# Eleven block products in place of twelve for units one to four, with w1 paired with w2, scores masked on two other engines, and the later steps listed anew

## The chip, the cores and the metric

The kernel runs on one NeuronCore of one Trainium2 chip. The metric is the device time of one execution in microseconds (us); less is better. The engines are named as the profile names them: PE is TensorE's matmul, PEld its weight load, DVE is VectorE, ACT is ScalarE, POOL is GpSimd, SP is SyncE, whose queue issues nearly all DMAs.

## The reference

Two blocks in a row, all in fp32. First a delta rule attention over 4 batches, 8 heads, 768 tokens and head size 48. For each batch and head, with k normalised to k_n:

```python
for t in range(S):
    y[:, :, t] = einsum('bhd,bhde->bhe', q[:, :, t], state)
    v_old = einsum('bhde,bhd->bhe', state, k_n[:, :, t])
    state = state + beta * einsum('bhd,bhe->bhde', k_n[:, :, t], v - v_old)
```

Then, on x = y laid out as 3072 tokens by 384 features, a feed-forward block: `h = ((x @ w1) * (x @ w2)) @ w3`, `out = h @ w_out`, with w1 and w2 of 384 by 1024, w3 of 1024 by 1024 and w_out of 1024 by 384.

## The kernel before

The attention works in 12 chunks of 64 tokens. A chunk has steps with names: `k`, `v` and `p` load its inputs, `d` turns permuted tiles of k and q into features (four DVE transposes into `KQ`), `s` forms scores on PE and takes from them U (scaled) and PT (masked by `smask`), `e` forms the off-diagonal corner of the chunk's inverse, `c` is the chain through the state (R = v minus old, then X, then the state S), and `y` forms outputs and copies them with ACT into `xT`, from which six DMAs move the last sixteen features of each row group. Two chunks make a unit of 512 tokens, numbered 0 to 5. Once for each unit `g` and `N` form the norms of k, and `V` inverts the 32 by 32 diagonal blocks by 31 pairs of DVE operations (L439, L444) on `Vb`, `Ub` and `tb`.

The feed-forward block follows unit by unit. w3 @ w_out is folded into `w34` at the start (L758), so a unit needs x @ w1, x @ w2, their elementwise product `ab`, and `ab` @ `w34`. The `a` steps form the two products for one of eight blocks of 128 columns at a time: three matmuls of 128 by 512 for w1, an ACT copy from PSUM, three for w2, and a DVE multiply from PSUM (L778, L790, L794). Unit 0 does it by halves of the tokens (`a` and `b` steps). The `o` step multiplies `ab` by `w34` with Winograd's seven products for eight; `S` (capital) forms its sums of `ab` on POOL (L1004), `T` its sums of weights, and `x` adds the results up from PSUM and stores them (L1032, L1063).

Unit 5, the last, has no attention beside it. Its `E` step already forms x @ w1 and x @ w2 by eleven products in place of twelve (L897): tokens in two halves, K in three parts, and Winograd's scheme over the first two parts and two halves of the columns, separately for w1 and for w2. `G` forms its token sums on DVE (L880) and `W` its weight sums on POOL (L858).

The PSUM has four single banks in turn, tag `f` (`ps_f`, for the feed-forward block), and two double banks, tag `w` (`ps_w`, for the attention).

What sets the order of the work: every step is a generator, and `ORDER`, one long list of names written out by hand, says which generator goes one `yield` further. At the end `in_text_order` ties each engine's instructions to the order of this text. So all queues are fixed, an engine that waits holds up all that is listed behind it on that engine, and only semaphores between engines decide when things start.

Of the kernel before, what the change touches and what calls it, by code (L numbers as in the profile page):

```python
# [8 lines left out]
FP32 = mybir.dt.float32  # L9
# [31 lines left out]
beta P12 g0 P3 K0 g0 K0 g0 P13 K1 g0 P8 P12 g0 K1 K1 P11 P9 Q0 Q0 g0 Q0 P10 P12 g0 Q0 Q0 g0 k2  # L41
K1 s0 g0 P9 P10 P8 N0 K1 q1 P2 s0 N0 P3 Q1 s0 P12 p2 g1 Q1 P2 N0 s0 s0 Q1 P9 Q1 P8 Q1 g1 s0 P3
s0 t2 t2 t3 s1 P5 P8 P2 g1 s1 P2 P1 s1 s1 t3 P9 P5 s1 P4 s1 P5 u0 P5 s1 d2 P1 P4 t1 u1 t0 P6 t4
P7 t1 t10 P1 t0 t5 V0 t4 P14 g1 V0 P1 t10 P6 f1 t5 V0 d2 P4 P6 V0 V0 V0 P7 V0 P7 V0 P16 P14 V0
P4 V0 P19 P19 P19 P6 f0 P16 P17 P17 V0 V0 P16 V0 V0 P17 P7 f2 k3 P14 p2 V0 V0 v1 P19 P15 f1 f0
g1 f1 t11 V0 d2 t11 P15 f2 f5 V0 P14 P15 f0 P16 v0 P17 V0 V0 V0 V0 g1 P20 f5 V0 f2 f5 t6 t9 P15
t6 P20 t7 V0 n1 P22 P20 V0 t7 d2 s0 V0 V0 f3 P23 P20 P22 t8 P21 V0 n0 P24 n0 f3 V0 V0 n1 t8 V0
V0 t9 V0 V0 s2 p3 f4 f3 P23 P22 P26 g1 V0 g1 V0 f4 g1 P21 P22 P23 t14 d3 f4 P23 g1 t12 p3 V0 N1
P30 t12 t14 t15 e0 t15 d3 f7 d3 f6 e0 P30 P21 e0 e0 P24 f7 s2 s2 e1 e0 s2 P24 e0 e1 V1 p4 s2 e1
P26 s2 e1 P25 d3 c0 P21 P30 u2 s3 c0 s3 P26 N1 P31 P24 y0 s3 s3 y0 c0 s3 s3 P25 t13 N1 e1 u3 P31  # L50
c0 P26 P31 P32 c1 V1 c1 e1 P25 V1 P27 c1 V1 c1 V1 V1 t13 V1 V1 V1 V1 V1 V1 y0 V1 P25 f7 f6 f6
P30 P32 P32 v2 V1 P27 s1 P31 V1 V1 y1 b3 b1 V1 b0 P32 P28 y1 b1 V1 b1 b3 P29 P27 b2 b3 y1 V1 P27
b1 b0 P29 P29 c1 a01 b2 a03 P28 V1 a01 a00 b3 P28 P29 a02 a02 a03 P35 P28 V1 a05 b7 a00 V1 V1 V1
V1 a06 P33 V1 b5 a05 b7 b0 V1 P34 V1 b5 V1 a06 V1 V1 V1 P34 k4 V1 P35 V1 g2 a00 V1 k5 a00 b0 V1
V1 g2 a04 P34 n2 p4 n2 a07 c1 a04 b2 b4 P33 b6 b2 P35 V1 g2 g2 P34 g2 e2 a07 g2 P33 e2 P35 c2 c2
e3 d4 a03 d4 a03 a01 P33 g2 b4 d4 g2 e2 b6 e2 a07 e2 b4 d4 T a01 T b4 e2 a07 c2 s4 p5 g2 c2 T g2
N2 V2 b6 p5 b6 s4 b5 s4 c2 a06 c2 a06 a04 v3 y2 d5 b5 d5 k6 s4 e3 d5 s4 y2 a02 a05 d5 s4 b7 a04
n3 S0 a02 a05 S0 s5 S0 u4 e3 s5 n3 s5 e3 b7 T o0 c3 c3 s5 g3 s5 S0 N2 N2 x0 e3 g3 e3 o0 s5 c3 c3
u5 o0 x0 V2 S0 x0 y3 V2 y3 S0 V2 S0 V2 S0 S0 V2 V2 V2 S0 g3 o0 S0 o0 S0 x0 V2 c3 o0 v4 y3 V2 V2
V2 x0 p6 V2 x0 V2 S0 a10 a10 S0 g3 S0 x0 V2 x0 S0 o0 x0 x0 p6 a14 V2 k7 a17 a17 a14 V2 V2 V2 a15  # L60
a16 V2 a16 a15 V2 g3 V2 V2 V2 V2 V2 v5 V2 x0 a13 V2 V2 V2 a17 a12 V2 a13 g3 V2 V2 g3 a17 c3 a14
a13 d6 d6 a11 V2 e4 n4 a12 e4 e4 c4 d6 V3 e4 a14 a10 n4 g3 d6 c4 e5 a11 e4 s6 g3 a13 e4 a12 p7
a10 c4 g3 N3 s6 c4 s6 a11 y4 n5 y4 c4 e5 a12 c4 a11 a15 c5 n5 e5 p7 a16 d7 d7 d7 d7 o1 c5 v6 a16
k8 g4 g4 e5 g4 p8 a15 g4 s7 s7 S1 e5 s7 S1 e5 x1 s7 s7 S1 s7 c5 o1 s6 S1 u7 c5 o1 s6 s6 u6 S1 S1
V3 S1 y5 c5 c5 V3 V3 V3 V3 V3 o1 S1 x1 k9 S1 y5 S1 y5 o1 S1 S1 x1 x1 V3 S1 S1 V3 c6 V3 S1 S1 V3
d8 o1 x1 x1 v7 a20 n6 x1 V3 a20 o1 x1 a23 V3 V3 x1 V3 x1 n7 a27 a24 d8 a26 V3 V3 V3 V3 x1 g4 V3
a23 V3 a25 V3 a27 a27 V3 a24 V3 V3 a26 a20 V3 g4 V3 p8 V3 V3 V3 V3 p9 V3 V3 a25 d8 n6 d8 g4 a20
a22 a22 a24 V3 c6 a27 a25 a24 a21 a21 e6 e6 e6 g4 e7 N3 e6 a25 N3 g4 s8 g4 N4 s8 e6 a22 s8 a26
e6 c6 c6 N4 s8 a26 s8 y6 a22 V4 p9 N4 S2 d9 e7 s8 a21 e7 y6 u8 d9 a21 e7 c6 a23 d9 p10 e7 d9 S2
c6 S2 s9 n7 a23 s9 e7 o2 s9 c7 s9 S2 s9 k10 S2 c7 x2 o2 c7 S2 S2 o2 u9 s9 V4 c7 V4 S2 y7 V4 V4  # L70
x2 V4 g5 g5 V4 p10 d10 y7 S2 x2 S2 o2 y7 V4 o2 x2 c7 V4 V4 S2 S2 V4 o2 a35 x2 x2 k11 x2 S2 V4 x2
S2 a35 v8 V4 S2 V4 V4 S2 V4 x2 n8 o2 a37 x2 V4 v9 V4 V4 V4 x2 a34 n8 V4 V4 a36 a30 V4 V4 V4 V4
V4 a37 V4 a34 a33 V4 g5 a33 a30 a32 a36 V4 V4 V4 V4 a34 a33 V4 V5 a32 e8 n9 c7 e8 a30 c8 a33 e8
e9 e8 g5 a35 a34 c8 a30 e8 g5 d10 a32 e9 g5 a32 g5 a36 e8 e9 S3 c8 a36 a35 a31 d10 d10 e9 a31 n9
c8 g5 c8 c8 g5 g5 e9 a31 s10 N5 e9 p11 s10 s10 a31 c9 a37 a37 p11 c9 y8 N5 v11 d11 S3 d11 d11 o3
v10 d11 s10 y8 s10 S3 u10 S3 s11 N5 s11 o3 s10 c9 s11 c9 s11 S3 x3 S3 s11 o3 S3 S3 y9 o3 s11 x3
S3 o3 u11 V5 S3 S3 V5 y9 V5 x3 n11 S3 x3 V5 V5 V5 S3 y9 S3 S3 V5 c9 V5 o3 x3 V5 x3 x3 V5 V5 x3
S3 a47 o3 x3 V5 V5 a47 x3 V5 V5 a47 n10 V5 a46 a40 a40 V5 a47 V5 a43 V5 a46 x3 a42 a45 V5 a42 V5
a41 a45 a43 V5 V5 V5 V5 V5 V5 a44 V5 a44 V5 a45 a41 V5 V5 V5 V5 c9 W W W W W W W W a42 e10 a40
e10 n11 a42 e10 a44 e10 c10 a45 n10 e11 e10 e11 c10 a43 e10 c10 c10 a40 e11 a41 a46 e11 c10 a44  # L80
S4 a43 e11 a41 S4 c10 o4 e11 a46 c11 x4 S4 S4 y10 o4 c11 c11 S4 y10 S4 S4 S4 S4 S4 c11 o4 y11 o4
x4 S4 S4 S4 o4 y11 x4 x4 o4 S4 x4 x4 S4 y11 S4 x4 G5 x4 E5 x4 o4 x4 E5 x4 E5 E5 S5 E5 E5 S5 E5
E5 S5 o5 S5 S5 S5 o5 S5 S5 S5 x5 S5 S5 S5 o5 o5 x5 S5 S5 S5 o5 S5 o5 x5 x5 o5 x5 x5 x5 x5 x5 x5
x5 x5 x5 x5
# [4 lines left out]
def kernel(  # L89
# [54 lines left out]

    def two_banks():
        return in_turn(psW, [P, 2, 512], "w", 2, "ps_w")
# [44 lines left out]
    kperm, qperm = (padded(x, [P, B, NP, 2, BS], 1)[0] for x in ("kperm", "qperm"))  # L191
# [3 lines left out]

    def load_crossed(src, m, dma, tag, bufs):

        t = in_turn(work, [P, NR, H, D], tag, bufs, tag)
        for z in range(2):
            for e in range(2):  # L200
                dma(  # L201
                    out=t[half(z ^ e)].rearrange("t r (a e) d -> t e (r a) d", e=2)[:, e],
                    in_=src.rearrange("(z r) (a e) t d -> z e (r a) t d", z=2, e=2)[
                        z, e, :, C * m : C * m + C, :
                    ].rearrange("g t d -> t g d"),
                )
        return t
# [14 lines left out]
    def load_perm(m):  # L222
        for src, dst in ((k, kperm), (q, qperm)):
# [15 lines left out]

    beta_tok = const.tile([P, NCH, NR, H], FP32, name="beta_tok")  # L240
# [4 lines left out]
    def across(src, dst):  # L245

        n = src.shape[1]
        ps = bank([P, n, NR, NP])
# [3 lines left out]
        psv = ps[:].rearrange("p c r a -> p (c r) a")  # L252
# [10 lines left out]
    def squares(j):  # L263
# [9 lines left out]
        yield from across(ss[:, 1], ss[:, 0])  # L273

    def norms(j):
# [31 lines left out]
        yield from across(w[:, 0], w[:, 1])  # L307
# [10 lines left out]
    def by_vector(m):  # L318
        KQ = new_KQ(m)
        for i, src in enumerate((kperm, qperm)):  # L320
            for z in range(2):
                bs = slice(NR * z, NR * z + NR)
                dve.transpose(
                    out=KQ[:, bs, :, i, :].rearrange("p b a t -> p (b a) t"),
                    in_=src[:, bs].rearrange("p b a x d -> p (b a) (x d)"),
                )
                yield
# [28 lines left out]
    def scores(m):  # L356
        u = Us[m % 2][:, 0 : NR * H * C].rearrange("p (r h t) -> p r h t", r=NR, h=H)
        for r in range(NR):
# [30 lines left out]
            if m < 2:  # L389
# [66 lines left out]
    T22s = padded("T22", [P, NR, H, BS], 2)  # L456

    def from_blocks(m):
# [6 lines left out]
        T22 = T22s[m % 2]  # L465
# [9 lines left out]
    def corner(m):  # L475
        yield from from_blocks(m)
        TT, T22, U, T11 = TTs[m % 2], T22s[m % 2], Us[m % 2], T11s[0]
# [64 lines left out]
    def chain(c):  # L542
        TT, nv, KQ = TTs[c % 2], vtoks[c], KQs[c]
# [21 lines left out]
        def by_features(ps, r, h, z):  # L565
            g = NP * r + h // 2
            return ps[feat(h % 2), z, D * g : D * g + D]
# [5 lines left out]
        R = nv  # L573
        if c > 0:
# [4 lines left out]
            R = in_turn(work, [P, NR, H, D], "R", 1, "R")  # L579
            v3, r3 = (  # L580
                x[:].rearrange("p r (a e) d -> p (r a) e d", e=2) for x in (nv, R)
            )
            dve.tensor_tensor(
                out=r3, in0=v3, in1=ps.rearrange("p e g d -> p g e d"), op=ALU.subtract
# [7 lines left out]
        for e in range(2):  # L592
            dve.tensor_tensor(
                out=X[:].rearrange("p r (a e) d -> p e (r a) d", e=2)[:, e], in0=ps[:, e],
                in1=scale_of(ws, c, 1).rearrange("p r (a e) -> p e (r a)", e=2)[:, e]
                .unsqueeze(2).to_broadcast([P, H, D]),
                op=ALU.mult,
            )
        yield
        if c < NCH - 1:  # L600
            kt = ktoks[c]
            ps = products(
                by_features,
                lambda r, h, z: kt[half((z + h) % 2), r, h, :],
# [4 lines left out]
            for z in range(2):  # L609
                f = feat(z)  # L610
                if c == 0:
                    dve.tensor_copy(out=Sn[f], in_=ps[f])
                else:
                    dve.tensor_tensor(out=Sn[f], in0=St[f], in1=ps[f], op=ALU.add)
# [73 lines left out]

    CW = 512
# [119 lines left out]
    def weight_sums():  # L809
# [11 lines left out]
        U3 = room[4][:, 0:DM]  # L821
# [12 lines left out]
    w12_sums = {}  # L834

    def w12_weight_sums():
        for w, (s, res) in enumerate(
            (
                (w1s, [new_room(x, [P, BS, BS], 1) for x in ("Ub", "Vb")]),
                (w2s, [kperm, qperm]),  # L840
            )
        ):
            flat = [
# [361 lines left out]
```

## Time and profile before

| what | value |
|---|---|
| three plain runs | 590.34, 588.90, 587.33 us; median 588.9 |
| the profiled execution | span 592.1 us, mean granted PE clock 0.971 |
| PE busy | 540.8 us (91%) |
| PEld busy | 393.3 us (66%) |
| DVE busy | 378.9 us (64%) |
| ACT busy | 159.2 us (27%) |
| POOL busy | 192.8 us (33%) |
| DMA | 57.32 MB, mean 97 GB/s |

The span of the profiled execution is 3.2 us over the median of the plain runs; what lies around the span is not in the profile. A matmul of this kernel is two passes in the records (288 records of L778 for w2 are 144 matmuls), and the mean duration of one record is longer than the distance of two, since passes overlap; the chain of waits shows the distance. Busy shares are averages over a start in which weights come in and a long middle in which attention and feed-forward share PE, so stages are read apart.

### The profile page before, as it was taken

How to read it: one execution, taken by the hardware profiler on the slowest of the kernel's cores; microseconds unless marked ns; L12 is line 12 of the kernel's file. 1: busy time of each engine (PE TensorE's matmuls, PEld its weight loads, DVE VectorE, ACT ScalarE, POOL GpSimd, SP SyncE). 2: the span in 40 equal slices, each digit the busy share in tenths (PEclk: the TensorE clock that was granted, in tenths of full speed). 3: DMA queues.
4: the chain of work that ended last, by engine and by line, in shares of the span. 5: the costliest groups of instructions: out<-in, count | busy, mean ns of one | idle time of the engine just before them, and what ended most of it. 6: DMA issues, size and time to landing. Idle time of an engine off the chain costs nothing.

```text
span 592.1 us, 19305 instructions
## 1 busy us (share of the span) xinstructions
PE 540.8 (91%) x8268; PEld 393.3 (66%) x8268; DVE 378.9 (64%) x872; ACT 159.2 (27%) x337; POOL 192.8 (33%) x240
## 2 busy tenths in 40 slices
PE   2469889788989999999999989999999999999997
PEld 2456455667878874558854659644688445988897
DVE  3796897678986579674787544874855943325432
ACT  4666354453412202121210222011122112311100
POOL 7563543032453701207121025022051071501441
PEclk9879998779999999999999989999999999999999
DMA  9979997677857445563453344625332040010001
GB/s 245 198 163 268 196 182 140 127 162 154 133 78 101 99 83 107 83 98 56 113 99 75 56 64 86 125 60 78 58 64 79 27 89 4 3 41 27 1 1 53
DMA packets 219508, 57.32 MB, mean 97 GB/s; under 512 B 206656, under 2 KB 212800, under 8 KB 219424
## 3 DMA queue, kind: packets, MB, share of 16 engines
q1 hardware_dynamic: 215232, 55.31, 47.2%
q10 hardware_dynamic: 4192, 0.79, 1.0%
q8 instruction: 65, 1.06, 0.8%
q14 instruction: 19, 0.16, 0.1%
HBM read 43.88 MB, written 11.01 MB: 93 GB/s over the span
## 4 chain that ended last, share of the span: by engine, by line
PE 60%; SPq 15%; DMA 14%; DVE 6%; issue 3%; ACT 1%; POOL 0%; DVEq 0%; ACTq 0%
PE ps_f L778 29%; PE ps_f L1032 14%; SPq L229 6%; PE ps_w L550 4%; DMA raw<-in_moe_w_dram 4%; PE ps_f L897 3%; PE ps_w L651 3%; PE ps_w L897 3%; DMA Ub<-Ud 2%; DMA ktok<-in_k_dram 2%; PE ps_w L497 2%; SPq L201 2%; DMA Ud<-U 2%; DVE tb L439 1%; SPq L683 1%
## 5 line engine op out<-in xcount | busy, mean ns | idle before, releaser
L778 PE MATMUL ps_f<-xT,w2s 128*128 128x512 f32 (+1 forms) x288 | 112.2, 535 | 2.2 <-issue 2.2
L778 PE MATMUL ps_f<-xT,w1s 128*128 128x512 f32 (+1 forms) x288 | 107.0, 524 | 2.8 <-DMA xT<-xT 2.8
L1004 POOL TENSOR_TENSOR ab<-ab 128x256 f32<-128x256 f32 x96 | 67.0, 728 | 90.2 <-DVE ab L794 60.9
L778 PEld LDWEIGHTS ps_f<-xT,w1s 128*128 128x128 f32 x288 | 53.9, 190 | 48.7 <-issue 42.9
L778 PEld LDWEIGHTS ps_f<-xT,w2s 128*128 128x128 f32 x288 | 53.4, 191 | 44.6 <-issue 41.5
L1032 PE MATMUL ps_f<-w,ab 128*128 128x192 f32 x376 | 66.6, 330 | 0.2 <-issue 0.2
L1032 PEld LDWEIGHTS ps_f<-w,ab 128*128 128x128 f32 x376 | 61.1, 190 | 3.8 <-issue 2.9
L790 ACT COPY ab<-ps_f 128x512 f32<-128x512 f32 (+1 forms) x48 | 23.6, 517 | 130.9 <-PE ps_f L778 119.6
L439 DVE TENSOR_TENSOR tb<-Vb,Ub 128x31 f32<-128x31 f32 (+15 forms) x124 | 44.8, 361 | 19.6 <-DMA Ub<-Ud 16.3
L1032 PE MATMUL ps_f<-room,ab 128*128 128x192 f32 x272 | 48.0, 329 | 1.0 <-DVE room L1063 0.8
L444 DVE TENSOR_TENSOR Vb<-Vb,tb 128x31 f32<-128x31 f32 (+15 forms) x124 | 45.0, 363 | 4.3
L758 PE MATMUL ps_f<-w2s,w3T 128*128 128x384 f32 x128 | 45.8, 513 | 0.2 <-ACT w3T L752 0.2
L1032 PEld LDWEIGHTS ps_f<-room,ab 128*128 128x128 f32 x272 | 44.1, 190 | 1.8 <-issue 1.3
L672 ACT COPY xT<-ps_w 48x256 f32<-48x256 f32 x96 | 30.4, 365 | 55.0 <-PE ps_w L651 54.5
L269 POOL TENSOR_TENSOR sq<-ktok 128x384 f32<-128x384 f32 x24 | 20.7, 868 | 68.6 <-DMA ktok<-in_k_dram 62.3
L794 DVE TENSOR_TENSOR ab<-ab,ps_f 128x512 f32<-128x512 f32 (+1 forms) x48 | 27.7, 590 | 16.9 <-PE ps_f L778 16.7
L536 POOL TENSOR_TENSOR vtok<-vtok,n 128x384 f32<-128x384 f32 x24 | 20.3, 855 | 50.1 <-DMA vtok<-in_v_dram 50.1
L758 PEld LDWEIGHTS ps_f<-w2s,w3T 128*128 128x128 f32 x128 | 25.0, 201 | 16.9 <-issue 2.4
L366 PE MATMUL ps_w<-KQ 48*64 48x128 f32 x384 | 30.1, 293 | 1.7 <-DVE PT L396 1.7
L372 PE MATMUL ps_w<-KQ 48*64 48x64 f32 x768 | 30.5, 232 | 0.1
L714 POOL TENSOR_TENSOR w<-w,raw 128x512 uint32<-128x512 uint32 x16 | 20.8, 1305 | 27.7 <-ACT raw L707 9.0
L372 PEld LDWEIGHTS ps_w<-KQ 48*64 48x64 f32 x768 | 27.3, 145 | 0.3 <-ACT KQ L346 0.2
(155 smaller groups left out, 782.2 us busy)
## 6 DMA issues: line engine op xcount, KB each, us to landing
raw<-in_moe_w_dram SPq DMA_DIRECT2D x16, 512.0 KB, 6.5
vtok<-in_v_dram SPq DMA_DIRECT2D x24, 192.0 KB, 4.4
raw<-in_moe_w_dram SPq DMA_DIRECT2D x24, 192.0 KB, 4.6
out_dram<-osb SPq DMA_DIRECT2D x46, 96.0 KB, 2.3
ktok<-in_k_dram SPq DMA_DIRECT2D x44, 96.0 KB, 4.2
raw<-in_moe_w_out_dram SPq DMA_DIRECT2D x8, 384.0 KB, 4.4
Ud<-U SPq DMA_DIRECT2D x48, 64.0 KB, 3.2
Ub<-Ud SPq DMA_DIRECT2D x6, 512.0 KB, 3.9
```

Of the source, the lines that this page charges most:

```text
L229: sync.dma_start(out=dst[quarter(2 * e + j), :, :, tb, 0:nd].rearrange("t b a d -> t (b a) d"), in_=src.rearrange("b (a e) t d -> e (b a) ...
L366: pe.matmul(ps[half(z), 0, n : n + 128], lhsT=x[:, 0, :], rhs=x.rearrange("p j t -> p (j t)"), start=True, stop=True,)
L372: pe.matmul(ps[half(z ^ j), 1, n + C * j : n + C * j + C], lhsT=x[:, 0, :], rhs=x[:, j, :], start=True, stop=True,)
L439: dve.tensor_tensor(out=tv, in0=V[:, 0 : s + 1, s : s + 1].to_broadcast([P, s + 1, n]), in1=U[:, s, s + 1 : BS].unsqueeze(1).to_broadcast( ...
L444: dve.tensor_tensor(out=o, in0=o, in1=tv, op=ALU.subtract)
L672: act.copy(out=xT[f, p:NP:2, b : b + NR, cc, :].rearrange("p a r t -> p r a t"), in_=pyv[f, z, b : b + NR],)
L758: pe.matmul(ps[:, 0:DM], lhsT=w3Ts[jc, kc // 4][:, kc % 4 * P : kc % 4 * P + P], rhs=wo[:, kc], start=(kc == 0), stop=(kc == KF - 1),)
L778: pe.matmul(ps[:].rearrange("p b c t -> p b (c t)"), lhsT=w[:, m, js], rhs=x[:, m, :, c0:c1].rearrange("p b c t -> p b (c t)"), start=(m = ...
L794: dve.tensor_tensor(out=t, in0=t, in1=ps, op=ALU.mult)
L897: pe.matmul(acc[i, w, name], lhsT=w12_sums[w][b][:, P * i : P * i + P], rhs=x_sums[u][x], start=new, stop=True, skip_group_check=not new,)
L1004: pool.tensor_tensor(out=o_, in0=x_, in1=y_, op=op)
L1032: pe.matmul(ps[b][:, b, :], lhsT=abs_[u, HF * f + i][:, t0 : t0 + P], rhs=ws_[w][:, i], start=first and i == 0 and (b == 0 or n == "F"), s ...
```

## The change

Units 1 to 4 get the eleven products too, and unit 5 is done in the same way. The scheme's column halves are now w1 and w2 themselves: for each pair `p` of column blocks (256 columns), B11, B21 and L1 are taken from w1 and B12, B22 and L2 from w2. Each of the eleven products is two matmuls of 128 by 256, both into one full bank of 128 by 512 (A, B, C or D). A unit has four such pairs, and a pair has four generators: `a` (P1 into A, an ACT copy, P6 and P7 into B with a DVE add after each), `h` (two rounds into C, three DVE operations), `i` (D, a DVE add, a POOL multiply by `late`) and `j` (P2 and L1 into A). Token sums are formed by POOL and the weight sums, 16 operations of 128 by 256, too. `S` works on 512 columns, 8 operations for a unit in place of 16. `o` and `x` are split by bank.

Besides: PT of chunks 4 to 11 is no longer a DVE multiply from PSUM but an ACT copy and a POOL multiply by `smask` (as for chunks 0 and 1). The state update is one DVE operation of 128 by 768 in place of two of 48 by 768, X one in place of two, and R overwrites v. To find room, `kperm` and `qperm` become one `perm` from chunk 4 on, used for k and then for q, with `spare` and `x_room` beside it, and `T22` is one tile from chunk 4 on. `across` uses a double bank from unit 3 on. `ORDER` is unchanged up to the middle of `V1` and is listed anew from there.

```diff
+    def perms(m):
+        if m >= 4:
+            return perm, perm
+        return perm, spare[:].rearrange("p (b a x d) -> p b a x d", b=B, a=NP, x=2)
...
-            if m < 2:
+            if m < 2 or m > 3:
                 act.copy(out=by_parity(PT), in_=psv[:, :, :, 1, :])
                 yield
                 pool.tensor_tensor(
...
-            for z in range(2):
-                f = feat(z)
-                if c == 0:
-                    dve.tensor_copy(out=Sn[f], in_=ps[f])
-                else:
-                    dve.tensor_tensor(out=Sn[f], in0=St[f], in1=ps[f], op=ALU.add)
+            if c == 0:
+                dve.tensor_copy(out=Sn[:], in_=ps)
+            else:
+                dve.tensor_tensor(out=Sn[:], in0=St[:], in1=ps, op=ALU.add)
...
+    def w12_parts(p):
+        n = HB * P
+        c = slice(n * p, n * p + n)
+        B11, B21, L1 = (w1s[:, m, c] for m in range(KM))
+        B12, B22, L2 = (w2s[:, m, c] for m in range(KM))
...
+    def token_sums(u):
+        for o_, x, y, op in token_parts(u)[1]:
+            pool.tensor_tensor(out=o_, in0=x, in1=y, op=op)
+        yield
...
+            for k, (x, b) in enumerate(todo):
+                for i in range(2):
+                    pe.matmul(
+                        acc[name][:, n * i : n * i + n],
+                        lhsT=ws[b][:, P * i : P * i + P], rhs=xs[x],
...
+        def main():
+            skip("f")
+            products("A", ("P1", "P1"))
+            yield
+            for z in range(2):
+                halves[u, p, z] = slab("ab")[:]
+            act.copy(out=halves[u, p, 1], in_=acc["A"])
+            yield
+            products("B", ("P6", "P6"))
+            yield
+            plus(halves[u, p, 0], halves[u, p, 1], "B")
+            yield
+            products("B", ("P7", "P7"))
+            yield
+            plus(halves[u, p, 1], halves[u, p, 1], "B")
+            yield
+
+        def second():
+            products("C", ("P5", "P5"), ("A2", "L2"))
+            yield
+            plus(late[:], halves[u, p, 1], "C")
+            yield
+            products("C", ("P3", "P3"), ("S5", "L2"))
+            yield
+            Z0 = halves[u, p, 0]
+            plus(Z0, Z0, "C")
+            yield
+            dve.tensor_tensor(out=Z0, in0=Z0, in1=acc["A"], op=ALU.mult)
+            yield
+
+        def other():
+            products("D", ("P4", "P4"), ("A2", "L1"))
+            yield
+            Z1 = halves[u, p, 1]
+            plus(Z1, Z1, "D")
+            yield
+            eng = dve if (u, p) == (last, HF - 1) else pool
+            eng.tensor_tensor(out=Z1, in0=Z1, in1=late[:], op=ALU.mult)
+            yield
+
+        def first():
+            products("A", ("P2", "P2"), ("A1", "L1"))
+            yield
...
-            for i in range(HF):
+            for i in range(HF if u == 0 else HF // 2):
```

## The prediction

> **What bounds the kernel now.** I read the page first, then the windows, then the chain of waits, then the groups by form, and the timeline where a duration looked odd.
>
> ```profile
> PE 540.8 (91%) x8268; PEld 393.3 (66%) x8268; DVE 378.9 (64%) x872; ACT 159.2 (27%) x337; POOL 192.8 (33%) x240
> ```
>
> 91% for PE is a mean over two stages. The windows (window, its length, then busy us and instructions of PE, PEld, DVE, ACT and POOL, the granted PE clock, DMA share and GB/s) part the middle, from the fourth chunk's outputs to the twelfth's, from the last unit:
>
> ```profile
> 203.50:519.60 316.10, 310.86 (x5021) 204.52 (x5017) 198.92 (x464) 60.78 (x136) 79.62 (x105) 0.99 0.39 72
> 519.60:588.80 69.20, 67.34 (x356) 61.46 (x352) 27.18 (x64) 7.96 (x22) 17.55 (x25) 1.00 0.06 18
> ```
>
> In both PE is busy 97 to 98% of the time; DVE has 63% in the middle, POOL 25%. So from 203 us on the time is PE's work, and each us taken off PE is a us of the run, until another engine holds PE up. The chain of waits (start, us, what) gives the price of that work, in passes (two to a matmul):
>
> ```profile
> 249.66 2.77 PE ps_f L778 x6
> ...
> 292.75 2.57 PE ps_f L778 x6
> ...
> 343.38 2.25 issue
> 345.62 4.54 PE ps_f L778 x6
> ...
> 538.75 1.73 PE ps_w L897 x8
> ```
>
> A pass of 512 columns takes 2.57/6 = 428 ns in a row, one of 256 columns 1.73/8 = 216 ns. After a burst of the attention's small matmuls, six passes take 2.77: a restart costs 0.20 us. The third piece is a stop of PE for 2.25 us, and behind it six passes took 4.54 where they take 2.77. The groups by form give the other prices (line, engine, shapes and count, then busy us and mean ns):
>
> ```profile
> L778 PE MATMUL ps_f<-xT,w2s 128*128 128x512 f32 x192 | 89.2, 610 | 2.2 <-issue 2.2
> L778 PE MATMUL ps_f<-xT,w1s 128*128 128x512 f32 x192 | 84.8, 594 | 0.5 <-DMA xT<-xT 0.5
> L1004 POOL TENSOR_TENSOR ab<-ab 128x256 f32<-128x256 f32 x96 | 67.0, 728 | 90.2 <-DVE ab L794 60.9 <-PE ps_f L1032 22.3 <-DVE ab L917 7.0
> L794 DVE TENSOR_TENSOR ab<-ab,ps_f 128x512 f32<-128x512 f32 x32 | 21.5, 681 | 16.5 <-PE ps_f L778 16.3
> L614 DVE TENSOR_TENSOR S<-S,ps_w 48x768 f32<-48x768 f32 x20 | 18.9, 947 | 11.7 <-PE ps_w L550 9.8 <-PE ps_f L254 1.7
> L396 DVE TENSOR_TENSOR PT<-ps_w,smask 128x512 f32<-128x512 f32 x20 | 13.5, 678 | 1.9 <-PE ps_w L651 1.9
> L392 POOL TENSOR_TENSOR PT<-PT,smask 128x512 f32<-128x512 f32 x4 | 5.1, 1275 | 2.5 <-DMA kperm<-in_k_dram 2.4 <-ACT PT L390 0.2
> ```
>
> **The products: -12.3.** Units 1 to 4 lose 384 passes of 512 columns, 384 x 0.428 = 164.5 us, and get 4 units x 4 pairs x 11 products x 2 matmuls x 2 passes = 704 passes of 256 columns, 704 x 0.216 = 152.2 us. By the ratio of columns alone, 1/12 of 164.5, it is -13.7; I take the rows. Weight loads double, but at 190 ns each they fit under a pass of 216 in the last unit, where the passes are of this kind already. That the change does what it says is seen in the listing: 440 matmuls of 128 by 256 where there were 88.
>
> **Finer mixing: +3.8.** A block's products used to go in threes; now pieces of two or four matmuls of 128 by 256 lie between attention steps. Counted in the two kernels' PE order from the fourth chunk's outputs on, the feed-forward work restarts behind small matmuls 55 times, 36 before: 19 x 0.20 = 3.8. Bounds: 0, where the small matmuls' own tail hides it, and 3.8.
>
> **Waits for DVE inside a pair: +1.0.** New is that PE waits for DVE in the middle of a sum: P7 goes into B only when the add has read P6 (and that add needs the ACT copy of A), the second round into C only when `late` is formed. Behind the waiting matmul stands all of PE's queue, attention included. The nearest row is the last unit, which did this already with eight sets of sums (waited for, us in total, times, longest us):
>
> ```profile
> PE ps_f L897 <- DVE ktok L908: 0.3, 1, 0.3
> ```
>
> Walking a pair in unit 5's new listing: P7 goes 1.7 us behind P6 (the first round of C between them, 8 passes), and the add takes 0.68; C's second round goes behind P7 and A's second products (1.73), and needs two DVE operations (1.36). So it fits, narrowly. In units 1 to 4 attention steps widen the gaps. With 0.3 us for eight sets, sixteen pairs cost 0.6; I take 1.0. Upper bound: 0.68 at each of 16 pairs, 11.
>
> DVE's load carries this. It gets 16 x 6 = 96 operations of 128 by 512 for 32, 64 x 0.68 = +43.5; loses 16 PT masks (-10.8), ten of twenty state updates (-9.5), and in X and the last unit some 3.4: 378.9 becomes 399. In the middle 198.9 becomes about 225 of 308 us, 73%. POOL gets per unit four PT masks and four multiplies at about 1.275, five token sums at 0.728, less 1.4 for the longer slab sums: +12.4 a unit, 25% becomes 42%. ACT gets 16 copies and loses 16: nothing. The weight sums (16 x 0.728 on POOL, 10 us for the 8 before) move from the end to the stretch ahead of unit 1's products; POOL was busy 28 of the 50 us from 150 on, which hides them; uncovered, unit 0's slab sums and `o` wait.
>
> POOL's load does reach DVE, in the timeline (start, us, instruction):
>
> ```profile
> 384.95 1.00 POOL L536 TENSOR_TENSOR vtok<-vtok,n 128x384 f32<-128x384 f32 x1
> 385.30 0.93 DVE L439 TENSOR_TENSOR tb<-Vb,Ub 128x247 f32<-128x247 f32 x1
> 385.91 1.00 POOL L269 TENSOR_TENSOR sq<-ktok 128x384 f32<-128x384 f32 x1
> ...
> 387.21 0.41 DVE L439 TENSOR_TENSOR tb<-Vb,Ub 128x240 f32<-128x240 f32 x1
> ```
>
> An inversion step takes 0.93 beside POOL and 0.41 without. An inversion is about 15 us a unit (90 over six); 12.4 us more POOL in 74 meets it for 2.5 us, so DVE gets up to 10 us more, 76%. It is off the path while PE has other work listed, so 0 beyond the 1.0.
>
> The Trainium skill speaks against the change here: "SBUF — State Buffer", section "Who interferes with whom", has a DVE operation with two SBUF inputs blocked by a GpSimd operation that reads SBUF, and one with a single SBUF input not. By that the new adds, which read PSUM, stay at 0.68 and only the inversion pays; the trace agrees, with 0.42 for an L908 of the last unit beside a POOL operation as without one.
>
> **SP: +0.5.** With one `perm`, the eight q loads of a chunk wait at SP for the two transposes of k, and DVE's transposes of q wait for their landing. SP took 4.1 us to issue eight (407.3), landing 2.7: 6.8 us. DVE's work listed between is 7 to 19 us for most chunks, but 2.1 between q of chunk 4 and k of chunk 5, and 5.0 within chunk 7: DVE may stand 4.7 + 1.8 us, and all that is listed behind it, adds and scores, with it. The single `T22` also makes SP wait for PE's `e` step. DVE stood 16 us for `Ub` loads in the middle before, and PE did not feel it; I take 0.5 of 0 to 6.5.
>
> **State update: -1.0.** One operation for two takes 0.95 us out of each chunk's recurrence, but PE seldom waits for it. The stop at 343.4 ended with the second L614 (343.76 to 345.63): with one, 0.95 less. Bounds: -4.0 (stop of 2.25 and slow passes of 1.77 both gone) and 0.
>
> **Sum.** -12.3 + 3.8 + 1.0 + 0.5 - 1.0 = -8.0, so a profiled span of 592.1 - 8.0 = 584.1. That execution was 3.2 over the median of the plain runs, so 588.9 - 8.0 = 580.9.
>
> **Rivals.** *More than forecast:* restarts hidden and the stop gone, -12.3 - 4.0 = -16.3, 572.6. For it: PE is the only bound, and the list is new. Against: the restart shows in every such row. *All given back:* DVE late by about 0.5 us at each of 16 pairs, -8.0 + 8.0, 588.9. For it: the narrow walk above; against: the 0.3 us row. *Slower:* PE stops once in each of units 1 to 4, while DVE is in an inversion or stands for `perm` and P7 waits, as long as at 343.4, and the clock falls as there (0.97 granted in that window of 50 us): 2.25 + 1.77 = 4.0 each, -8.0 + 16 = +8, 597. It decides from the third such stop on, two being break-even. For it: DVE at 76% in fixed order, with PE tied to it; against: before, with DVE at 63%, it was one stop in 316 us.
>
> The Trainium skill, "TensorE: Matmul & The Clock Gate", Part 1, halves the clock only after an idle window of about 3.4 us; by that, four stops of 2.25 us would cost 9 and the run end near 590. The row decides: 2.25 us were enough.
>
> **How the numbers follow.** Forecast 0.51 (574 to 586), more 0.11, given back 0.12, slower 0.26. The range leaves out some 4% below 571 and 9% above 598. About 0.5%, 2.9 us, is what a measurement of this kernel can tell: the forecast and the better case are faster, 0.62; the case that gives all back is the same, 0.11, but for 0.01 of it, which with the slower case makes 0.27.
>
> **What would show it.** In the profile after: 704 more passes of 128 by 256 at 216 ns, PE's busy time down by some 8 to 12 us; DVE near 400 us, POOL near 245; waits of PE for DVE's adds of a few us in all, and no granted clock under 0.99 from 203 us on. Wrong if PE has gaps of over 2 us behind those adds or slow passes behind them, if the start (until 200 us) is longer, or if 256-column passes among attention steps take more than 216 ns.

## The result and the profile after

The changed kernel takes 631.8 us (median of 4 runs, 629.0 to 636.5) where the kernel before takes 589.6 (4 runs beside it): 1.073 times as long, 95% interval 1.067 to 1.080. It was forecast at 580.9. Medians and ratios, here and below, leave out the few runs that fell in a slower state of the chip. The profiled execution spans 630.2 us, 38.1 more than the one before; the medians are 42.2 apart, since the profiled execution of the kernel before was a long one. The page's first part:

```profile
PE 550.9 (87%) x8588; PEld 464.0 (74%) x8588; DVE 435.6 (69%) x870; ACT 158.1 (25%) x329; POOL 248.4 (39%) x263
```

The 320 added passes are there, but PE is busy 10 us more, not 8 to 12 less. POOL is where it was expected (245), DVE 37 us above its 399. The windows, cut where the fourth and the twelfth chunk's outputs end (columns as in the prediction):

```profile
0.00:215.60 215.60, 169.91 (x2965) 130.74 (x2965) 157.39 (x344) 93.28 (x183) 100.10 (x119) 0.93 0.73 155
215.60:558.50 342.90, 313.48 (x5273) 271.78 (x5273) 255.39 (x490) 58.93 (x132) 130.45 (x129) 0.96 0.35 65
558.50:630.20 71.70, 67.47 (x352) 61.50 (x352) 22.81 (x37) 5.85 (x14) 17.88 (x17) 0.99 0.08 25
```

The last unit is as before (71.7 for 72.5). The start is 12.1 us longer, and the middle takes 342.9 us for 316.1, with PE idle for 29 us of it and its clock at 0.96. The chain of waits shows that the products cost what the sum said: 0.218 us a pass in the last unit.

```profile
571.19 36.60 PE ps_f L919 x168
```

The waits of PE say where it stopped (line waited for: us in total, times, longest):

```profile
PE ps_f L1029 <- POOL x_room L905: 12.6, 2, 6.3
PE ps_f L1029 <- DVE room L1059: 11.1, 2, 6.3
...
PE ps_f L919 <- DVE ab L927: 1.9, 2, 1.4
```

Within the pairs PE waited 1.9 us for the adds, where 1.0 was forecast. The 23.7 us are four stops of 4.8, 6.3, 6.4 and 6.2 us, one at the end of each of units 0 to 3, all at the same matmul: T3 of the `o` step, the second product into bank B. It may start when DVE has read T2 out of that bank, by the first add of `xB` (U2, L1059). Two of the stops are put down to POOL's token sums, which ended at the same moment; but T3 does not read those, and in both cases the U2 add had ended 0.15 us ahead of PE's start. The timeline at the end of unit 1 (start, us, instruction; POOL, DVE and PE):

```profile
297.12 5.26 POOL L1000 TENSOR_TENSOR ab<-ab 128x512 f32<-128x512 f32 x4 [5.64 <-PE ps_f L1029]
...
296.80 0.32 DVE L461 TENSOR_TENSOR tb<-Vb,Ub 128x156 f32<-128x156 f32 x1
297.15 1.42 DVE L466 TENSOR_TENSOR Vb<-Vb,tb 128x156 f32<-128x156 f32 x1
...
302.63 1.31 DVE L466 TENSOR_TENSOR Vb<-Vb,tb 128x192 f32<-128x192 f32 x1
...
308.52 0.41 DVE L461 TENSOR_TENSOR tb<-Vb,Ub 128x240 f32<-128x240 f32 x1
...
311.11 0.55 DVE L1059 TENSOR_TENSOR room<-room,ps_f 128x384 f32<-128x384 f32 x1
...
311.80 5.46 PE L1029 MATMUL ps_f<-room,ab 128*128 128x192 f32 x16 [6.31 <-DVE room L1059]
```

An inversion operation takes 0.32 us alone and 1.3 beside POOL's slab sums, as long as one of those (5.26 / 4 = 1.32). The U2 add stands on DVE behind 14 inversion steps, two operations each. The kernel before has 5 such steps there (6, 5, 6 and 2 at the four boundaries, where the changed kernel has 13, 14, 13 and 10). And behind the stop, sixteen passes take 5.46 us; at 294.8 us, at full clock, sixteen take 2.87. The groups by form:

```profile
L1000 POOL TENSOR_TENSOR ab<-ab 128x512 f32<-128x512 f32 x40 | 50.9, 1298 | 56.0 <-PE ps_f L1029 43.8 <-DVE ab L966 11.7
L927 DVE TENSOR_TENSOR ab<-ab,ps_f 128x512 f32<-128x512 f32 x80 | 54.4, 682 | 42.2 <-PE ps_f L919 40.0 <-ACT ab L935 1.4
```

The new adds, which read one operand from PSUM, keep their 0.68 us beside POOL, as forecast (683 ns for the 24 that lie wholly beside a POOL instruction, 683 for the 70 that touch none). The inversions of units 2 to 5 do not: 126.8 us (their operations summed) for 89.8, the 37 us that DVE has too much. For 66 us of that time POOL is busy too, before it was 8: the new list puts the slab sums, the token sums and some masks beside the inversion, where the old one had started the inversion behind the sums.

From here on a *stretch* is the time from the first to the last operation of one inversion of units 2 to 5. The windows over the stretches, the second one and the sum over four, of the changed kernel:

```profile
294.00:333.60 39.60, 33.17 (x260) 30.71 (x253) 35.85 (x74) 4.58 (x12) 14.85 (x14) 0.91 0.31 55
...
sum 162.70, PE 134.48 PEld 122.44 DVE 150.70 ACT 16.95 POOL 71.01; mean PE 33.62 PEld 30.61 DVE 37.67 ACT 4.24 POOL 17.75
```

and of the kernel before:

```profile
285.80:316.30 30.50, 30.50 (x164) 18.33 (x164) 26.25 (x70) 3.51 (x6) 3.47 (x4) 1.00 0.45 81
...
sum 118.30, PE 117.53 PEld 72.69 DVE 102.48 ACT 17.92 POOL 9.96; mean PE 29.38 PEld 18.17 DVE 25.62 ACT 4.48 POOL 2.49
```

Before, PE was busy through the stretches and DVE had slack; after, DVE is busy 93% of them and PE waits. So 38.1 us are +12.1 in the start, +44.4 in the four stretches, and -18.4 in the rest of the time behind the start (414.6 - 162.7 = 251.9 for 388.6 - 118.3 = 270.3). The experiments ask which of these is cause.

### The profile page after: what moved, and what is told of

The parts are those of the page before. It is cut to its first block, busy times and chain, and to the rows that moved or that the text cites. A ratio compares the mean times of both kernels' runs of the same rounds, so it can differ in the third digit from the quotient of the medians.

```text
span 630.2 us, 19989 instructions
## 1 busy us (share of the span) xinstructions
PE 550.9 (87%) x8588; PEld 464.0 (74%) x8588; DVE 435.6 (69%) x870; ACT 158.1 (25%) x329; POOL 248.4 (39%) x263
## 4 chain that ended last, share of the span: by engine, by line
PE 57%; DVE 12%; SPq 12%; DMA 11%; issue 3%; ACT 2%; POOL 2%; DVEq 0%; POOLq 0%; ACTq 0%
PE ps_f L919 29%; PE ps_f L1029 13%; PE ps_w L578 4%; DVE tb L461 4%; SPq L249 4%; DMA raw<-in_moe_w_dram 3%; DVE Vb L466 3%; PE ps_w L674 3%; SPq L706 2%; PE ps_w L525 2%; DMA Ub<-Ud 2%; PE ps_f L799 2%; PE ps_w L388 2%; PE ps_w L394 1%; DMA ktok<-in_k_dram 1%
## 5 line engine op out<-in xcount | busy, mean ns | idle before, releaser
L1000 POOL TENSOR_TENSOR ab<-ab 128x512 f32<-128x512 f32 (+1 forms) x56 | 62.5, 1143 | 56.4 <-PE ps_f L1029 44.2
L927 DVE TENSOR_TENSOR ab<-ab,ps_f 128x512 f32<-128x512 f32 x80 | 54.4, 682 | 42.2 <-PE ps_f L919 40.0
L919 PE MATMUL ps_f<-xT,w1s 128*128 128x256 f32 x320 | 79.4, 383 | 0.0
L1029 PE MATMUL ps_f<-room,ab 128*128 128x192 f32 x272 | 56.1, 368 | 23.7 <-POOL x_room L905 12.6
L966 POOL TENSOR_TENSOR ab<-ab,late 128x512 f32<-128x512 f32 x19 | 24.2, 1274 | 88.6 <-DVE ab L927 87.1
L414 POOL TENSOR_TENSOR PT<-PT,smask 128x512 f32<-128x512 f32 x20 | 26.2, 1310 | 56.8 <-ACT PT L412 56.8
L919 PE MATMUL ps_f<-xT,room 128*128 128x256 f32 x160 | 41.5, 390 | 2.9 <-DVE ab L927 1.9
L919 PE MATMUL ps_f<-xT,w2s 128*128 128x256 f32 x160 | 40.9, 383 | 0.0
L919 PE MATMUL ps_f<-x_room,w2s 128*128 128x256 f32 x160 | 39.1, 387 | 0.4 <-DVE late L927 0.3
L919 PEld LDWEIGHTS ps_f<-xT,room 128*128 128x128 f32 x160 | 29.0, 189 | 9.2 <-issue 2.3
L919 PEld LDWEIGHTS ps_f<-x_room,w2s 128*128 128x128 f32 x160 | 29.2, 190 | 6.6 <-DVE late L927 2.1
```

The source lines that it names most:

```text
L414: pool.tensor_tensor(out=PT, in0=PT, in1=smask[:].unsqueeze(1).to_broadcast([P, H, C]), op=ALU.mult)
L919: pe.matmul(acc[name][:, n * i : n * i + n], lhsT=ws[b][:, P * i : P * i + P], rhs=xs[x], start=new and k == 0 and i == 0, stop=k == len(t ...
L927: dve.tensor_tensor(out=o_, in0=x, in1=acc[name], op=ALU.add)
L966: eng.tensor_tensor(out=Z1, in0=Z1, in1=late[:], op=ALU.mult)
L1000: pool.tensor_tensor(out=o_, in0=x_, in1=y_, op=op)
L1029: pe.matmul(ps[b][:, b, :], lhsT=block(u, HF * f + i, z)[:, P * b : P * b + P], rhs=ws_[w][:, i], start=first and i == 0 and (b == 0 or n ...
```

## The experiments

Each time is a median; each ratio, with its 95% interval, compares all the runs (not the medians) with those of the kernel before on the same chip.

**First round.** Theory A: PE stops because the U2 add stands behind inversion steps that POOL's sums slow down. Rivals: the list is late whatever POOL does (B), or the masks are to blame (C).

*Without the slab sums.* In `slab_sums`:

```diff
-                pool.tensor_tensor(out=o_, in0=x_, in1=y_, op=op)
+                if u > 3:
+                    pool.tensor_tensor(out=o_, in0=x_, in1=y_, op=op)
```

> The changed kernel without GpSimd's slab sums of units 0 to 3 (this work is left out; the second products read ab unsummed); every order stays as it is. Theory A: the inversion operations beside them fall from 1.3 us to 0.3, DVE loses about 25 us, the U2 add comes 3.4, 7, 6 and 6.5 us earlier, and about 2 of the 23.7 us of stops are left; with the slow passes minus 25 to minus 32, 600 to 607 us. Rival B (the listing alone, with 28 inversion operations ahead of the U2 add, is late whatever GpSimd does): stops of 4 us and more remain at each boundary, minus 5 to minus 10, 622 to 627.

602.7 us (1.022 times the kernel before, 1.014 to 1.029), as theory A had it. The inversions fell to 99.1 us, PE's stops from 203 us on to 7.7 us in all, and the stretches:

```profile
sum 133.20, PE 125.18 PEld 113.56 DVE 123.11 ACT 17.01 POOL 36.33; mean PE 31.30 PEld 28.39 DVE 30.78 ACT 4.25 POOL 9.08
```

*The U2 add ahead of 6 to 9 steps* (`V2` and so on moved behind `xB0` in `ORDER`, for units 0 to 3).

> The changed kernel with one difference: at the boundaries behind units 0 to 3 the U2 add (the first step of xB) is listed on DVE ahead of the last 6, 7, 7 and 9 of the inversion steps that stand before it; all work and every other order stay. Theory A (PE's four stops of 4.8, 6.3, 6.4 and 6.2 us come from the U2 add being listed behind inversion steps that run at 1.3 us an operation beside GpSimd's slab sums): the inversions stay as slow (about 125 us of DVE), but the stops shrink to under 6 us together and the slow passes behind them (8.4 us) go too; minus 20 to minus 32, 600 to 612 us. Rival B (DVE simply has too much to do, 436 us of 630): no work is taken away, so the waits only move to the next add; 625 to 634.

640.7 us (1.083; 1.076 to 1.091): slower. At T3 PE no longer waits, but at the next add it does, 9 us long in two places, for the steps moved there stand ahead of that one. The timeline of DVE, and of PE at the end of unit 2:

```profile
409.15 0.55 DVE L1059 TENSOR_TENSOR room<-room,ps_f 128x384 f32<-128x384 f32 x1
409.80 0.55 DVE L1059 TENSOR_TENSOR osb<-room,ps_f 128x384 f32<-128x384 f32 x1
...
410.50 5.07 PE L1029 MATMUL ps_f<-w,ab 128*128 128x192 f32 x16 [9.45 <-DVE osb L1059]
```

So the place of that one add is not the cause. This spoke for rival B.

*Masks back on DVE* (`if m < 2 or m > 3:` becomes `if m < 2:`).

> The changed kernel with PT of chunks 4 to 11 masked by DVE again, in one multiply from PSUM, in place of the ScalarE copy and the GpSimd multiply. DVE gets 16 x 0.68 = 11 us, GpSimd loses 16 x 1.31 = 21, of which 8 lie beside inversions. Theory A: the masks are a small part of what lies beside the inversions ahead of the U2 add (about 1 us at two of the boundaries), so 626 to 633 us, about no change. Rival C (the masks on two engines are the cause): the time falls by over 15 us.

633.1 us (1.074; 1.067 to 1.081), as the changed kernel: the masks on two engines cost nothing by themselves, and rival C is out. The stretches became 5 us shorter in sum, and PE waited 3.6 us for PT elsewhere.

*POOL adds beside the inversions of the kernel before.* In `inverse`, behind the second step of units 2 to 5 (shortened):

```diff
+            if j >= 2 and s == 1:                # x: 512 columns of Ub; idle: unused columns of a room
+                pool.tensor_copy(out=idle[:, 0:1], in_=t[:, 0:1])
+                for i in range(6):
+                    pool.tensor_tensor(out=idle, in0=x, in1=x, op=ALU.add)
```

> The kernel before with six GpSimd adds of 128 by 512 more (into an idle tile, their result is not used) started by the second step of each inversion of units 2 to 5: 7.7 us of GpSimd each, beside the inversion steps that stand ahead of the U2 add. Theory A: about six inversion operations take 1.3 us for 0.25, DVE comes to the U2 add some 6 us later, of which it had 2.2 and 0.4 us to spare at the two boundaries looked at; PE stops 3 to 5 us at each boundary and runs slow behind it: plus 12 to plus 28, 601 to 617 us. Rival (an inversion slowed beside GpSimd is hidden, since PE has other work listed): under plus 3, at most 592.

624.4 us (1.058; 1.053 to 1.063), more than expected, and not by the expected way alone: an inversion operation beside the adds took 1.08 us, and the inversions 112 us for 90, but PE's four stops (23.6 us) were put down to POOL's slab sums, which now stood behind the added work. It shows that the kernel before has no room for 7 us in its stretches, not through which engine.

**Second round.** If slow steps are the cause, spreading them or taking POOL's sums away from them should help.

*Steps spread behind the next unit's pairs* (`ORDER` alone: 36 steps, up to two at a time, behind the DVE steps of `a`, `h` and `i`), *sums on DVE*, and *both*:

```diff
-                pool.tensor_tensor(out=o_, in0=x_, in1=y_, op=op)
+                eng = dve if u < last else pool
+                eng.tensor_tensor(out=o_, in0=x_, in1=y_, op=op)
```

> The changed kernel with inversion steps listed elsewhere and nothing else changed: those taken out ahead of the U2 add (6, 7, 7, 9 at the boundaries of units 0 to 3) and between U2 and the next xB add (1, 0, 3, 3) do not go right behind it, as in the last listing, but one to two at a time behind the DVE steps of the next unit's pairs. Theory A (PE stops at whichever x add stands behind inversion steps that are slow beside GpSimd): fewer steps stand beside the slab sums, so DVE's inversions cost some 10 to 20 us less than 127, and no x add has more than three steps ahead of it; stops at the boundaries under 8 us together for 26, 600 to 612 us. Rival B (too much DVE work, so the steps hold up the next thing wherever they go): new waits for the adds within the pairs or for the inverse itself, 620 to 640.

> The changed kernel with the slab sums of units 0 to 4 on DVE in place of GpSimd, all orders as they are. DVE gets 16 operations of 128 by 256 at some 0.4 us and 32 of 128 by 512 at some 0.7, 29 us in all, but no inversion step stands beside them: by theory A it loses the 25 us that the inversions were slower, so its busy time stays near 436 while the wait ahead of the U2 add shrinks by about 3 us a boundary, and a sum takes PE's products 0.7 in place of 1.3 us; 606 to 620 us. Rival B (DVE's volume counts, GpSimd's help does not matter): 29 us more on DVE make it slower, 632 to 650.

> Both edits together: the slab sums of units 0 to 4 on DVE, and the inversion steps taken out ahead of the x adds and spread behind the DVE steps of the next unit's pairs. Theory A: neither contention nor a long row of steps stands ahead of an x add; stops at the boundaries under 5 us, about as the kernel without slab sums (602.7) or a little less, 595 to 606. Rival B: as either edit alone, above 615.

636.1 (1.075; 1.066 to 1.084), 634.9 (1.075; 1.068 to 1.082) and 634.4 us (1.076; 1.067 to 1.084): three misses for theory A. With the steps spread, the adds of `xB` stand behind about as many inversion steps as in the kernel before (U2 behind 7, 7, 6 and 1, the next behind 10, 10, 9 and 4, for 6, 5, 6, 2 and 10, 9, 9, 7), so their place in the list alone is not the cause. No stop at T3 is left, but 22.6 us of waits for the adds within the pairs, which now stand behind inversion steps. With the sums on DVE the inversions fell to 101 us, and the sums took the place of what was gained. The stretches:

```profile
sum 164.40, PE 135.00 PEld 121.96 DVE 141.92 ACT 16.86 POOL 37.39; mean PE 33.75 PEld 30.49 DVE 35.48 ACT 4.21 POOL 9.35
```

162.7 before the edit, 164.4 with it. Compare the kernel without sums, where neither engine does them: 133.2.

*Fills in place of the adds* (`pool.memset(idle, 0.0)` sixteen times, in the kernel before):

> The kernel before with sixteen GpSimd fills of 128 by 512 (8.3 us, they write SBUF and read nothing) in the place of the six adds of 7.7 us started by the second step of each inversion of units 2 to 5. If what slows the inversions is GpSimd reading SBUF, as with the adds, the inversion operations beside the fills keep their 0.25 to 0.35 us and the time stays at 588 to 594. If any work of GpSimd on SBUF does it, they take about 0.6 us and more, and the time goes to 605 to 625.

636.3 us (1.077; 1.066 to 1.088; two runs), where 588 to 594 was expected if fills do not slow the steps, though the inversions took 94.5 us, little more than the 90 without. The timeline:

```profile
391.79 9.25 POOL L449 MEMSET room<- 128x512 f32 x16
...
392.36 0.28 DVE L439 TENSOR_TENSOR tb<-Vb,Ub 128x112 f32<-128x112 f32 x1
```

Four operations ran beside the fills, at their usual 0.25 to 0.28 us; then DVE stood 8.9 us for a POOL product queued behind the fills, and PE 33.7 us for the slab sums queued there. So fills do not slow the inversion, as far as four operations can tell, and the time was lost in POOL's queue.

**Third round.** Theory D, formed from this: in a stretch DVE has no idle time to speak of, PE has a fixed amount of listed work, and whatever lengthens the stretch beyond that is lost.

*Without the inversion steps of units 2 to 5*, in the changed kernel and in the kernel before:

```diff
         for s in range(BS - 1):
+            if j >= 2:
+                yield
+                continue
```

> The changed kernel without the DVE steps of the inversions of units 2 to 5 (left out: the blocks then count as their own inverse); everything else stays, GpSimd's slab sums too. New theory D: from the first to the last step of an inversion DVE has no idle time, and PE, whose list in that stretch now needs more DVE operations, waits for it; the stretch is 39 to 45 us in the changed kernel and 26 to 32 before (sum over four: 162.7 and 118.3 us), and that difference of 44 is the loss. Without the steps PE alone bounds: 578 to 594 us. Rival E (GpSimd's sums, masks and late multiplies, or the order of the o and x steps, hold PE up whatever DVE does): over 605.

> The kernel before without the same DVE steps of units 2 to 5. Theory D: there PE has work beside every inversion already, so only its few stops go: 581 to 590 us. If the kernel before were bound by DVE in those stretches as well, it would fall below 575.

592.7 (1.005; 1.002 to 1.009) and 590.8 us (1.002; 0.999 to 1.005; a shade over the 581 to 590 expected). The same steps are worth 39 us in the one kernel and nothing in the other. POOL's sums, masks and late multiplies are all still there. The middle of the changed kernel without them and of the kernel before without them, and the longest wait of PE for DVE in the first:

```profile
215.60:519.40 303.80, 302.63 (x5273) 263.95 (x5274) 139.87 (x250) 58.83 (x132) 124.28 (x129) 1.00 0.40 73
...
203.30:516.00 312.70, 308.75 (x5017) 204.22 (x5017) 112.66 (x216) 60.79 (x136) 78.58 (x104) 1.00 0.40 73
```
```profile
PE ps_f L922 <- DVE late L930: 0.4, 2, 0.2
```

PE is busy 99.6% of the changed kernel's middle, at full clock, and the middle takes 303.8 us. Like is compared with like when the steps are out of both kernels: 303.8 for 312.7, 8.9 us less. That is what the products (-12.3) and the finer mixing (+3.8) promised together, once DVE is free. (The 316.1 of the kernel before with its steps holds the stop at 343 us and its slow passes besides.)

*Pairs 0 and 2 by twelve products again*, with 2 DVE operations a pair in place of 6, and token sums behind pair 2; and the same with the steps spread. (w2's first third stays as the weight sums leave it, so these products are not the reference's; their number and shapes are.) In outline:

```diff
+    def twelve(u, p):                       # for p in (0, 2) of units 1 to 4; per half z of the tokens:
+            ps = product(w1s, z)            # 6 matmuls of 128 by 256
+            act.copy(out=t, in_=ps)
+            ps = product(w2s, z)
+            dve.tensor_tensor(out=t, in0=t, in1=ps, op=ALU.mult)
```

> The changed kernel with pairs 0 and 2 of units 1 to 4, those whose products run beside the inversion, formed by twelve products again (per half of the tokens six matmuls of 128 by 256 for w1, an ACT copy, six for w2, one DVE multiply): 2 DVE operations a pair for 6, one GpSimd multiply less, 48 passes for 44. The token sums move behind pair 2. PE gets 8 x 4 x 0.216 = 7 us more. Theory D: the stretches of the inversion lose about 5 us of DVE each and the token sums beside them, 8 x 0.68 and some 2: 162.7 becomes about 135, and the time falls by some 27 less 7: 604 to 618 us. Rival E: no gain, 630 to 640.

> As the last, and the inversion steps taken out ahead of the U2 add and between it and the next xB add (6, 7, 7, 9 and 1, 0, 3, 3) are spread behind DVE steps of the next pairs. Theory D: with fewer pair operations in the stretch the spread steps no longer hold the pairs up, and fewer of them stand beside the slab sums: 598 to 614 us. If the steps again only move the waits, about as the last or slower.

642.9 (1.092; 1.088 to 1.095) and 641.8 us (1.089; 1.084 to 1.094): misses. The stretches did not shrink (165.7 and 164.6 us): fewer DVE operations stood in them, but DVE stood idle for 28 and 37 us of them (12 in the changed kernel), much of it waiting for PE's products, whose places in the list had changed. DVE's sum of work is thus a floor for a stretch, not its length.

**Fourth round: two doses.** Every third, or every sixth, inversion step left out (`if j >= 2 and s % 3 == 2`, `s % 6 == 5`).

> The changed kernel with every third step of the inversions of units 2 to 5 left out (10 of 31). Theory D as a threshold: in the stretch from an inversion's first to its last step PE has about 30 us of listed work (without the steps the run lost nothing there: 375.8 us from the fourth chunk's outputs on, where the changed kernel takes 414.6, so 38.8 / 4 = 9.7 a stretch, and DVE needs 39.6 busy us in a stretch on average). A third less inversion is about 10 us less, 29.5: the loss is all but gone, span 591 to 600. If the loss goes in proportion to the inversion work, a third of 38.8 comes back: about 617.

> The changed kernel with every sixth step of the inversions of units 2 to 5 left out (5 of 31), some 5 us a stretch. Theory D as a threshold: DVE needs 35.2, 32.6, 32.3 and 38.5 us in the four stretches, PE has about 30, so some 18 us of the loss of 38.8 are left: span 605 to 614. In proportion: 630 - 6 = 624.

606.0 (1.025; 1.018 to 1.032; span 605.0) and 620.4 us (1.048; 1.043 to 1.054; span 622.4): between the two expectations in both. The steps left took longer beside POOL, so the inversions fell by 30 and 16 us in sum and not by 40 and 20. Taken against what fell, by the medians: the first 16 us taken out bring 11 back, the next 14 bring 14, and the other 97 (all steps gone) 13. That is a threshold.

All runs together settle what holds. For each: the sum of the four stretches, the time from the end of the fourth chunk's outputs to the end of the profiled execution, and the difference (all worked out from the timelines):

| kernel | stretches | from outputs 4 to the end | difference |
|---|---|---|---|
| before | 118.3 | 388.6 | 270.3 |
| before, POOL adds | 151.3 | 422.3 | 271.0 |
| before, POOL fills | 162.2 | 433.4 | 271.2 |
| changed | 162.7 | 414.6 | 251.9 |
| U2 ahead | 172.6 | 424.7 | 252.1 |
| steps spread | 168.6 | 421.4 | 252.8 |
| sums on DVE | 164.4 | 419.4 | 255.0 |
| both | 166.5 | 419.1 | 252.6 |
| no slab sums | 133.2 | 387.6 | 254.4 |
| a third out | 135.1 | 389.8 | 254.7 |
| a sixth out | 150.4 | 405.6 | 255.2 |
| masks on DVE | 157.4 | 415.7 | 258.3 |
| mixed, mixed and spread | 165.7, 164.6 | 426.3, 426.8 | 260.6, 262.2 |

Outside the stretches little changes: 270 to 271 us with the old products, 252 to 255 with the new (also in the four kernels of the fifth round, 251.7 to 252.4); the masks on DVE add the waits for PT, the mixed kernels their 32 more passes (8 pairs x 4 x 0.216 = 6.9 us). Without any inversion the same list takes 375.8 us, so PE has 375.8 - 252 = 124 us of work in the four stretches, 31 each. The changed kernel's stretches last 40.7 on average. Of the 38.8 us between the two, PE is idle for 28.2 (162.7 - 134.5), and 10.5 are its 124 us of work taking 134.5, with the slow passes behind the stops. No run has the new products, all the work, and an order in which DVE's work in a stretch stays below PE's; whether the change could pay with another list is open.

**Fifth round: the start.** The list of the kernel before up to the first `o`, in the changed kernel; then with two tiles for k and q of chunks 4 and 5 (`if m >= 6: return perm, perm`); two tiles in the new list; and two tiles with the q loads listed where the kernel before has them.

> The changed kernel with its steps listed as in the kernel before from the middle of V1 up to the first o step of unit 0 (with the two loads into the single perm put behind the transposes that they wait for), and in the new order from there on; the work is that of the changed kernel. If the new listing makes the start longer (the fourth chunk's outputs end at 215.6 us in the changed kernel, 203.5 before), they end at 203 to 208 and the run loses 8 to 12 us: 618 to 625. If the edits do it (masks by ScalarE and GpSimd, one perm, one T22), they stay at 211 or later and the time at 627 to 635.

> The last listing (start as in the kernel before, the new order from the first o step on), and chunks 4 and 5 with two tiles for the permuted k and q again (spare holds q until the third set of weight sums needs it). In the last run PE waited 5.7 and 4.0 us in the start for DVE's transposes, which waited for q to land in the single perm. If the single perm is what makes the old start impossible, the fourth chunk's outputs end at 203 to 209 us for 225, and the run ends 16 to 22 us earlier than the last: 619 to 626. If the masks or the merged steps do it, they end above 215 and the time stays above 630.

> The changed kernel in its own order with two tiles for the permuted k and q of chunks 4 and 5. If the new listing has paid for the single perm in the start by its order, two tiles alone give little: the fourth chunk's outputs at 210 to 216 us, time 626 to 634. If the single perm itself makes the start longer in this order too, they end at 208 or earlier and the time falls by 6 us or more.

> As the run with the old start and two tiles for chunks 4 and 5, but the q loads of both chunks are listed where the kernel before has them, ahead of the transposes of k (in the last two runs of the old start they stood behind those, as the single perm needs it, and PE still waited 5.3 us for the transposes of q). If the single perm, with the late q loads that come with it, is the reason why the old start does not fit the changed kernel, the wait goes and the fourth chunk's outputs end at 205 to 213 us for 219, the run at 618 to 626. If they stay at 217 or later, masks, the merged steps or the seam between the two lists do it.

The fourth chunk's outputs ended at 225.2, 219.1, 214.8 and 211.8 us (215.6 in the changed kernel, 203.5 before), the runs took 641.0 (1.083; 1.078 to 1.088; above both of its ranges), 635.0 (1.075; 1.071 to 1.079), 629.2 (1.066; 1.061 to 1.072) and 625.2 us (1.059; 1.053 to 1.065). In the first, PE stood for the transposes of the single `perm`:

```profile
175.08 0.65 PE L388 MATMUL ps_w<-KQ 48*64 48x128 f32 x2 [5.67 <-DVE KQ L345]
```

So in the old order the single tile, with the q loads that it makes late, costs 225.2 - 211.8 = 13.4 us; in the new order 0.8. The new list exists in part because of it. But 8 of the 12 us stay with two tiles and the old order, and what they are is not settled: the masks of chunks 4 and 5, the merged steps and the seam between the two lists are left. The last of these kernels is the fastest with the new products and all work done, still 35 us behind the kernel before.

## Why the prediction was wrong

**Products, -12.3, and finer mixing, +3.8: right together.** With DVE out of the way in both kernels the middle is 8.9 us shorter, for 8.5 in the sum; no run parts the two.

**Waits inside a pair, +1.0: about right**, 1.9 us for the adds.

**DVE's load: this step failed, twice.** The prediction saw an inversion step slow down beside POOL (0.93 for 0.41) and priced it at up to 10 us of DVE in all, "off the path while PE has other work listed, so 0 beyond the 1.0". The size was wrong because POOL's work was taken as spread evenly; the list puts it beside the inversion, 66 us of overlap for 8, and DVE needed 37 us more. (It also divided the 90 us of inversion by six units; they are those of units 2 to 5, 22 us each, which would have made its 10 us 15.) That it is off the path was wrong too: without the inversion steps the run is 39 us shorter. One mean over 316 us (DVE 63%, then 73%) hid the stretches: 87% busy before (102.5 of 118.3), with about 4 us of slack in each. The end of each unit was not walked at all, only the inside of a pair.

**The slower rival** had the mechanism half right: PE stops once a unit behind an inversion, and the clock falls. It put the stop at P7, where the waits came to 1.9 us in all; it came at T3, behind `xB`, and it was priced at 2.25 + 1.77 where it was 4.8 to 6.4 plus 1.6 to 2.6 (sixteen passes took 4.4 to 5.5 us for 2.87). Its 597 was a fifth of the way.

**One `perm`, +0.5, bound 6.5:** right in the new order (0.8), and 13.4 in the old one, above the bound. **The start** was taken as unchanged, with the weight sums the only thing priced there; it cost 12, part of which is open. **State update, -1.0:** no run isolates it. The kernel before without inversion steps still stops there for 1.8 us and the changed kernel without them does not, but its list is new as well.

The Trainium skill, "SBUF — State Buffer", "Who interferes with whom", says that a DVE operation with two SBUF inputs contends with a GpSimd instruction that reads SBUF, and not with one that only writes it. The runs agree in each part, and a blocked operation took as long as the GpSimd instruction beside it: 1.31 us beside sums of 1.32, 1.08 beside adds of 1.11 (6.64 / 6), 0.28 beside fills (four operations). The prediction cited the rule and then multiplied it by the wrong overlap.

## What to carry to other kernels

Price contention with the order of the lists, not with mean loads: for each long row of DVE steps, read what POOL has listed beside it and which PSUM bank is freed behind it. Where PE needs a second engine within a stretch, compare that engine's work in the stretch with PE's listed work there; here DVE's steps cost nothing as long as its work stayed below PE's (590.8 us without them, 589.5 with them), above that most of each us counted (25 of the first 30 taken out came back), and moving the work about in the same stretch gave nothing back. An experiment that leaves a whole suspect out (39 us in one kernel, none in the other) tells more than several that move it.

## What the hardware did that was not expected

The clock after a stop of PE. The length of a stop does not decide whether slow passes follow: behind a stop of 2.02 us (every third step left out, at 219.1 us) the granted clock fell, behind stops of 2.73 (the same run, 298.9) and 3.21 us (every sixth left out, 220.6) it did not. The clock records show what goes with it. In all twenty traces the granted clock is 1.0 or 0.5, and changes only on a grid of 3.41 us. Take the windows of that grid from 200 us on that have the clock at 1.0 and PE idle for at least a fifth: all 68 windows with PE idle for 59% or more are followed by a window at 0.5, and of the 83 with less only 8 are. The stop of 2.02 us made a window 59% idle; the one of 3.21 us lay across two windows, 43 and 51% idle. The 2.25 us of the prediction made its window 66% idle; the same place without inversion steps, 1.78 us across two windows, 27 and 25% idle, has no slow passes. So whether a stop of about 2 us costs slow passes is in part the luck of where it falls; each of the four stops of the changed kernel made a window over 75% idle. The Trainium skill, "TensorE: Matmul & The Clock Gate", Part 1, has the clock watched in free-running windows of about 3.4 us, which the grid agrees with, and halved after an idle window; in these runs 59% of a window was enough.
